# Sliding-window attention and gated FFN, gradients: the mean of dO.V without a block-sum matmul, and some of the order changed

## The chip, the cores and the metric

The kernel runs on one core of one Trainium2 chip. The metric is device time in microseconds (us), given as the median of three runs. Engines are named as in the profile: PE is TensorE's matmuls, PEld its weight loads, DVE is VectorE, ACT is ScalarE, POOL is GpSimd, SP is SyncE, which here only issues DMAs. L12 is line 12 of the kernel before.

## The reference

The forward pass mixes two branches of x (2048 rows of 512, bf16) by a gate of each row: `out = g*a + (1-g)*b` with `g = sigmoid(sum(x * gate_w))`. Branch a is attention with 32 heads of 16 lanes, in which row s sees rows s-255 to s; branch b is a FFN of width 1376 in which the gate passes a ReLU.

```
qkv = x @ wqkv
scores = q @ k.T / 4 ; keys with 0 <= i - j < 256 ; p = softmax(scores) ; a = (p @ v) @ wo
gate = relu(x @ W_gate) ; up = x @ W_up ; b = (gate * up) @ W_down
out = g * a + (1 - g) * b
results: out and the gradients of x, wqkv, wo, W_gate, W_up, W_down, gate_w for a given grad_out
```

For the gradient of the scores each query needs `dP - D`, where dP is dO.V for each key and D is the mean of dO.V under the row's softmax, which equals the sum over the 16 lanes of dO times O. D is the subject of the main part of the change.

## The kernel before

**How work is written.** Python first collects operations (an `Op` has the engines that may do it with a cost on each, the buffers it reads and writes, and a rank), then `Flow.run` plays them against its own costs, L261 on: at each moment each free engine takes the ready operation of lowest rank that finds buffers and PSUM banks, and its instructions are emitted there. So each engine's order of instructions is fixed when the program is built, and at run time each engine takes them in that order and waits where data are not there. Where PE has nothing ready and has been idle lately, a filler matmul is emitted (L1504). The ranks of PE's operations between 3.4 and 4.3 (front and back of the FFN, some weight gradients, projections) get a random part of up to 0.02 from a fixed seed (L295 to L298).

**How attention is tiled.** Four heads make a group, 4 row blocks of 128 make a sub-block of 512 rows, and a stage is one group in one sub-block: 8 groups x 4 sub-blocks = 32 stages. Each head has 32 lanes: 16 of k or q ("lo") and 16 of v or dO ("hi"). A stage of kind A (dq side: rows are keys, columns queries) and one of kind N (dk/dv side: rows are queries, columns keys) follow each other: A of stage n, then N of stage n-1. `pack_queries` and `pack_keys` (L27) cut a stage's pairs of blocks into three packs of up to 4 blocks of 128 columns; a pack is a list of segments (row block, first column block, count), and a segment is one matmul for a head. For two of the four heads a pack makes a unit, so a stage has six units.

Each unit passes twice through `slot` (L1018): first its scores (L995, "row" matmuls of 32 rows, four at a time in the array) go through Exp on ACT (L1037) and a mask on POOL (L1013), and some slots later dP is made by L995 again from the operands `dd` and `kv1`, and multiplied by p on DVE (L1043). The masks cover runs of diagonal and far blocks, one instruction a run. Sweeps (L1063, "col" matmuls of 32 or 16 columns) multiply by v, k, q and dO and sum up over the packs. All other matmuls are "den": L662 for the projections, the FFN and weight gradients, L1346 for dx, out and the second half of the FFN.

**The chain to `dd`**, once in a stage (`tasks_A1`, L1072 to L1102): a sweep makes O and the softmax sums in PSUM (`LO`); a shuffle on DVE (L1087), Ln and Exp on ACT (L1088, L1089) give the reciprocals `ri`; DVE writes `OB`, the normalised O in the hi lanes (L1090); `U = ri * qd` is made on POOL or DVE (L1092); `pr = OB * U` (L1094) on POOL or DVE. A matmul with the constant `bones` (L1096) sums pr over a head's lanes and leaves -1/16 of the sum in its lo lanes, in the PSUM bank `de`. DVE makes `dd = U * is_hi + de` (L1098). Since `kv1` holds ones in the lo lanes, the dP matmul takes D off by itself. U is also turned by a DMA transpose on SP into `R` (L1100), which N's sweeps use, rank 1. Units of kind N of stage n-1 whose queries lie in the next sub-block need `dd` and the queries of stage n.

**The last part.** `dw(c)` (L1245) makes the gradients of wqkv and wo for a quarter of the columns: SP turns the stored head rows into `RW`, then 64 matmuls of 384 columns and 16 of 512; dw(0) and dw(1) have ranks 4.05 and 4.5, dw(2) and dw(3) 4.7. `early` (L1354) makes the FFN's parts for row blocks 0 to 11 and stores them (b_d, dx_p). `final` (L1417) then loads those (`b_t`, `x_t`, L1423 and L1424) and a pair's head rows `qk` (`load_heads`, L1319, L1324: four loads of 256 KB for two row blocks, `HQ` names the queues), multiplies by the weights wT3 (loaded at L1378 by SP) and wo, and ACT, POOL and DVE add up, o and dx are stored by SP (L1444, L1450). `whole` (L1453) does blocks 12 to 15 without the store between. The loads of qk, b_t and x_t may go on the queue of SP or of ACT, whichever `Flow.run` finds free.

Of the kernel before, what the change touches and what calls it, by code (L numbers as in the profile page):

```python
# [26 lines left out]
def pack_keys(i, nt):  # L27

    packs = [[(i + 2, i, 3), (i, i, 1)], [(i + 4, i + 2, 2), (i + 1, i, 2)], [(i + 5, i + 3, 1), (i + 3, i + 1, 3)]]
    return [place([s for s in p if s[0] < nt], lambda a, b: a - b) for p in packs]  # L30
# [20 lines left out]
HOLD, WAIT = 2.5, 800  # L51
SEED = 32
SPAN, LOW, NEED, PHASE = 3413.3, 3000, 3600, 0

def t_mm(count, cols=512):
    return count * (cols / 2.4 + 3)
# [146 lines left out]
class Flow:  # L203
# [57 lines left out]
    def run(self):  # L261
# [32 lines left out]

        rnd = random.Random(SEED)  # L295
        for o in self.ops:
            if PE in o.times and o.mode != "row" and 3.4 < o.rank < 4.3:
                o.rank += rnd.uniform(0, 0.02)  # L298

        def release(ops):  # L300
# [87 lines left out]
def kernel(  # L388
# [21 lines left out]
    P = 128  # L410
# [20 lines left out]
    MASKQ, MASKV = {DVE: 450, ACTE: 600}, {DVE: 470, ACTE: 600}  # L431
    DTT = 640
    FUSED = 0
    HQ, OUTS, GLAG = (SP, ACTE), 2, 3
    COLX, ROWX = 20, 4
# [36 lines left out]
    for w in range(2):  # L472
# [3 lines left out]
                                base=16 * w + 15, pattern=[[32, 4]], channel_multiplier=-1)  # L476
    head_m = mc.tile([P, 4], F32, name="head_m")
    nc.vector.tensor_tensor(out=head_m[:], in0=lo_m[:, :, 0], in1=lo_m[:, :, 1], op=ALU.add)
    vec = mc.tile([P, 4], F32, name="vec")
# [6 lines left out]
    less_hi = vec[:, 3:4]  # L486
    bones = mc.tile([P, 4, 2, 16], BF, name="bones")
    nc.gpsimd.memset(bones[:], 0.0)
    nc.vector.tensor_scalar(bones[:, :, 0, :], bc(head_m[:], 16), -1.0 / Dh, None, op0=ALU.mult)
    g_all = mc.tile([P, NT], F32, name="g_all")  # L490
# [581 lines left out]
    def tasks_A1(n, us):  # L1072

        hg, sb = divmod(n, NSB)
        LO, de = (buf("acc") for _ in range(2))
        ri, OB, U, pr, R = (buf(nm) for nm in ("ri", "OB", "U", "pr", "R"))
        dd, qd = st["in", n][2], st["qd", n]

        def w1(a, i):
            d, k = divmod(a - 4 * sb, 4)  # L1080
            return st["k1r", n + d][:, k, 32 * i:32 * i + 32]

        def b1(segs):
            return [st["k1r", n + (s_[0] - 4 * sb) // 4] for _, s_ in segs]

        sweep(LO, us, w1, b1, False, [OB], rank=RC)
        op({DVE: t_dve(W)}, lambda e: nc.vector.stream_shuffle(ri[:], LO[:], 2 * list(range(16))), r=[LO], w=[ri], rank=RC)  # L1087
        op({ACTE: t_act(W)}, lambda e: nc.scalar.activation(ri[:], ri[:], ACT.Ln), r=[ri], w=[ri], rank=RC)  # L1088
        op({ACTE: t_scale(W)}, lambda e: nc.scalar.activation(ri[:], ri[:], ACT.Exp, scale=less_hi), r=[ri], w=[ri], rank=RC)  # L1089
        op({DVE: t_stt(W)}, lambda e: nc.vector.scalar_tensor_tensor(  # L1090
            out=OB[:], in0=LO[:], scalar=is_hi, in1=ri[:], op0=ALU.mult, op1=ALU.mult), r=[LO, ri], w=[OB], rank=RC)
        op({POOL: t_pool(W, 2), DVE: t_dve(W)}, lambda e: EN[e].tensor_tensor(  # L1092
            out=U[:], in0=ri[:], in1=qd[:], op=ALU.mult), r=[ri, qd], w=[U], rank=RC)
        op({POOL: t_pool(W, 2), DVE: DTT}, lambda e: EN[e].tensor_tensor(  # L1094
            out=pr[:], in0=OB[:], in1=U[:], op=ALU.mult), r=[OB, U], w=[pr], rank=RC)
        op({PE: t_mm(1)}, lambda e: nc.tensor.matmul(de[:], lhsT=bones[:].rearrange("p a b c -> p (a b c)"), rhs=pr[:],  # L1096
                                                     start=True, stop=True), r=[pr], w=[de], rank=RC, mode="den", keep=[dd])
        op({DVE: t_stt(W)}, lambda e: nc.vector.scalar_tensor_tensor(  # L1098
            out=dd[:], in0=U[:], scalar=is_hi, in1=de[:], op0=ALU.mult, op1=ALU.add), r=[U, de], w=[dd], rank=RC)
        dma(lambda: nc.sync.dma_start_transpose(out=R[:], in_=U[:]), r=[U], w=[R], nbytes=128 * KB, rank=1, turn=True)  # L1100
        put(OB, *divmod(hg, 2), sb, 0, 1, 2)
        st["rn", n] = R  # L1102
# [142 lines left out]
    def dw(c):  # L1245
# [16 lines left out]
        for cd in range(DC):  # L1262
            bank, dwst = buf("mm"), buf("dwst")
            mms = [mm(lambda bank=bank: bank[:, 0:3 * P], lambda t=t, cd=cd: x_r[:, t, cd * P:(cd + 1) * P],
                      lambda t=t: RW[:, t, P:4 * P]) for t in range(NT)]
            accumulate(bank, mms, [RW, x_r], DW if c < 2 else DW2, [dwst], cols=3 * P)

            def out(e, bank=bank, dwst=dwst):
# [10 lines left out]
        accumulate(bank, [mm(lambda: bank[:], lambda t=t: Or[:, t, :], lambda t=t: db_r[:, t, :]) for t in range(NT)],  # L1279
                   [Or, db_r], DWO if c < 2 else DW2, [dst])  # L1280
        op(either(W), lambda e: copy(e, dst[:], bank[:]), r=[bank], w=[dst], rank=2)
# [135 lines left out]
    def final(t, qk):  # L1417
# [4 lines left out]
        b_t, x_t = buf("b_t"), buf("x_t")  # L1422
        dma(lambda q: q.dma_start(b_t[:], b_d[t][:]), r=[b_d[t]], w=[b_t], nbytes=256 * KB, rank=3.15, on=(SP, ACTE))  # L1423
        dma(lambda q: q.dma_start(x_t[:], dx_p[t][:]), r=[dx_p[t]], w=[x_t], nbytes=256 * KB, rank=3.15, on=(SP, ACTE))  # L1424
        dxb = buf("tb")
# [107 lines left out]
```

## Time and profile before

| what | value |
|---|---|
| median of 3 runs | 848.98 us (848.01 to 849.01) |
| profiled execution, its own time | 851.36 us |
| its span, first to last instruction | 849.7 us |
| granted clock of PE, mean of the span | 0.994 |
| PE, DVE, ACT, POOL busy | 97%, 82%, 72%, 64% |
| DMA | 152.17 MB, mean 179 GB/s |
| L1096, the block-sum matmul | x32, 381 ns a record |
| L1094, the product pr | 23 on DVE (575 ns), 9 on POOL (1153 ns) |
| L1098, dd | x32 on DVE, 738 ns |

The span has three parts: up to about 40 us the first loads and projections, then attention stages with FFN and projection matmuls between them up to about 720 us (slots of L995, sweeps of L1063, the rest of PE's time filled by L662 and later L1346), and from there the end, in which PE runs L1346, the last dw and little else. A matmul's record is longer than the distance between two starts, since they are pipelined, so a matmul's price is read from starts. Idle time of an engine other than PE costs only where PE comes to wait for it.

### The profile page before, as it was taken

What the parts mean: (1) busy time and instruction counts of PE and PEld (TensorE: products, weight loads), DVE (VectorE), ACT (ScalarE), POOL (GpSimd) and SP (SyncE); (2) the same over time, 40 slices, a digit from 0 to 9 for tenths busy, and PEclk for the clock granted to TensorE, in tenths of its full rate; (3) what the DMA queues carried; (4) which work ended last, traced back from release to release, by engine and by line L of the source; (5) the groups of instructions that cost most, each with busy time, mean ns of one, the idle gap of its engine ahead of it and who ended that gap; (6) DMA issues with size and microseconds to landing.
All of it is one profiled execution on the core that took longest, in us unless ns stands there. A gap on an engine that the chain in (4) does not pass through costs nothing.

```text
span 849.7 us, 24038 instructions
## 1 busy us (share of the span) xinstructions
PE 823.5 (97%) x8722; PEld 372.8 (44%) x8722; DVE 698.6 (82%) x1278; ACT 614.8 (72%) x1244; POOL 544.0 (64%) x942
## 2 busy tenths in 40 slices
PE   8999999999999999999999999999999999999999
PEld 5433444434454544445354444443333333444444
DVE  5589899898999797999999998988989899634351
ACT  5778887797888787888888798988887877321232
POOL 6378677687798586978867685556565665122341
PEclk9999999999999999999999999999999999999999
DMA  8978565656678888878875599537656464889892
GB/s 230 227 169 207 143 159 139 140 155 156 147 197 187 171 196 176 194 171 208 192 169 154 158 222 205 147 103 153 177 147 171 138 184 154 251 255 278 245 229 60
DMA packets 317033, 152.17 MB, mean 179 GB/s; under 512 B 205233, under 2 KB 309234, under 8 KB 316274
## 3 DMA queue, kind: packets, MB, share of 16 engines
q1 hardware_dynamic: 297090, 135.69, 65.5%
q10 hardware_dynamic: 19248, 13.37, 5.3%
q0 software_dynamic: 576, 1.57, 0.8%
q8 instruction: 68, 1.11, 0.6%
q14 instruction: 51, 0.42, 0.2%
HBM read 55.02 MB, written 55.74 MB: 130 GB/s over the span
## 4 chain that ended last, share of the span: by engine, by line
PE 73%; DMA 10%; POOL 5%; DVE 5%; ACT 3%; issue 2%; SPq 1%; ACTq 0%; DVEq 0%; POOLq 0%
PE banks L662 34%; PE banks L1346 17%; PE banks L995 12%; PE banks L1063 8%; DVE arena L1043 2%; POOL arena L1013 2%; ACT arena L1037 2%; POOL arena L868 1%; DMA arena<-HD_d 1%; DMA arena<-arena 1%; DMA ffn_d<-arena 1%; DMA QD_d<-arena 1%; DMA arena<-QD_d 1%; DMA arena<-KV_d 1%; PE banks L1096 1%
## 5 line engine op out<-in xcount | busy, mean ns | idle before, releaser
L1043 DVE TENSOR_TENSOR arena<-arena,banks 128x512 bf16<-128x512 bf16 (+2 forms) x768 | 461.3, 645 | 39.0 <-PE banks L995 29.4
L1013 POOL TENSOR_SCALAR_AFFINE_SELECT arena<-arena 128x256 bf16<-128x256 bf16 (+1 forms) x736 | 350.2, 499 | 180.9 <-ACT arena L1037 163.8
L1037 ACT ACTIVATE arena<-banks 128x512 bf16<-128x512 f32 (+2 forms) x768 | 399.8, 573 | 81.4 <-PE banks L995 71.9
L662 PE MATMUL banks<-arena 128*128 128x512 bf16 (+4 forms) x1984 | 392.7, 337 | 4.7 <-DVE arena L1043 2.2
L662 PEld LDWEIGHTS <-arena 128*128 128x128 bf16 (+1 forms) x1984 | 174.0, 99 | 160.9 <-issue 61.8
L1346 PE MATMUL banks<-arena 128*128 128x512 bf16 (+1 forms) x784 | 186.6, 380 | 2.4 <-DMA arena<-wt_d 1.7
L995 PE MATMUL banks<-arena 32*128 32x384 bf16 (+2 forms) x2816 | 166.6, 277 | 8.4 <-DVE arena L1043 2.0
L995 PEld LDWEIGHTS <-arena 32*128 32x128 bf16 x2816 | 51.5, 92 | 157.7 <-issue 147.2
L640 ACT CAST arena<-banks 128x512 bf16<-128x512 f32 (+4 forms) x167 | 81.0, 497 | 53.9 <-PE banks L662 42.0
L868 POOL TENSOR_TENSOR arena<-arena 128x512 bf16<-128x512 bf16 (+1 forms) x84 | 98.4, 1176 | 20.7 <-DVE arena L863 10.8
L1346 PEld LDWEIGHTS <-arena 128*128 128x128 bf16 (+1 forms) x784 | 69.8, 97 | 93.9 <-issue 20.3
L1063 PE MATMUL banks<-arena 128*32 128x384 bf16 (+5 forms) x2816 | 103.0, 277 | 4.3 <-DMA arena<-arena 3.3
L1063 PEld LDWEIGHTS <-arena 128*32 128x32 bf16 (+1 forms) x2816 | 57.6, 94 | 42.0 <-issue 24.6
L1442 POOL TENSOR_TENSOR arena<-arena 128x512 bf16<-128x512 f32 x12 | 15.2, 1266 | 49.5 <-ACT arena L1441 27.0
L1092 POOL TENSOR_TENSOR arena<-arena 128x512 bf16<-128x512 f32 x31 | 36.1, 1165 | 9.4 <-issue 7.2
L868 DVE TENSOR_TENSOR arena<-arena 128x512 bf16<-128x512 bf16 (+1 forms) x48 | 36.7, 767 | 2.6 <-DMA ffn_d<-arena 2.2
L1446 DVE SCALAR_TENSOR_TENSOR arena<-gw_b,arena 128x512 f32<-128x512 bf16 x12 | 10.4, 865 | 25.6 <-ACT arena L1445 25.6
L1448 POOL TENSOR_TENSOR arena<-arena 128x512 bf16<-128x512 f32 x12 | 15.5, 1305 | 24.1 <-DMA out_dram<-arena 15.0
L863 DVE SCALAR_TENSOR_TENSOR arena<-arena,banks 128x512 bf16<-128x512 bf16 (+1 forms) x44 | 29.7, 677 | 0.9 <-PE banks L662 0.8
L1441 ACT ACTIVATE arena<-banks,g_all 128x512 f32<-128x512 f32 x12 | 8.1, 686 | 30.8 <-PE banks L1346 13.2
L1445 ACT COPY arena<-banks 128x512 f32<-128x512 f32 x12 | 6.9, 584 | 26.4 <-PE banks L1346 23.9
L858 ACT ACTIVATE arena<-banks 128x512 bf16<-128x512 f32 (+1 forms) x36 | 21.7, 604 | 5.4 <-PE banks L662 4.4
(92 smaller groups left out, 459.8 us busy)
## 6 DMA issues: line engine op xcount, KB each, us to landing
ffn_d<-arena SPq DMA_DIRECT2D x40, 384.0 KB
arena<-ffn_d SPq DMA_DIRECT2D x88, 128.0 KB
out_dram<-arena SPq DMA_DIRECT2D x66, 128.0 KB
arena<-HD_d ACTq DMA_DIRECT2D x31, 256.0 KB
KV_d<-arena SPq DMA_DIRECT2D x32, 128.0 KB
QD_d<-arena SPq DMA_DIRECT2D x32, 128.0 KB
arena<-KV_d SPq DMA_DIRECT2D x32, 128.0 KB
arena<-QD_d SPq DMA_DIRECT2D x32, 128.0 KB
```

The costliest lines, as they stand in the source:

```text
L640: nc.scalar.copy(out, in_)
L662: return lambda start, stop: nc.tensor.matmul(out_fn(), lhsT=lhs_fn(), rhs=rhs_fn(), start=start, stop=stop)
L858: nc.scalar.activation(q["rg"][:fs, :], gps[:fs, :], ACT.Relu)
L863: op({DVE: t_stt(W)}, lambda e, q=q, ups=ups: nc.vector.scalar_tensor_tensor(out=q["upm"][:fs, :], in0=q["rg"][:fs, :], scalar=0.0, in1=up ...
L868: op({POOL: t_pool(W, 2), DVE: DTT}, lambda e, q=q, k=k, a=a, b=b: EN[e].tensor_tensor(out=q["act"][:fs, k, :], in0=q[a][:fs, :], in1=q[b] ...
L995: nc.tensor.matmul(bank, lhsT=lt[rs, ls], rhs=rt[rs, rsl], start=True, stop=True)
L1013: nc.gpsimd.affine_select(out=v.rearrange("p h (b k) -> p h b k", b=cnt), in_=v.rearrange("p h (b k) -> p h b k", b=cnt), compare_op=ALU.i ...
L1037: op({ACTE: t_act(w)}, lambda e, h=h: nc.scalar.activation(nxt.Pt[:, h, :w], nxt.S[h][:, :w], ACT.Exp), r=[nxt.S[h]], w=[(nxt.Pt, h)], rank=0)
L1043: op({DVE: t_dve(wc)}, lambda e, h=h: nc.vector.tensor_tensor(out=cur.Pd[:, h, :wc], in0=cur.Pt[:, h, :wc], in1=cur.dP[h][:, :wc], op=ALU. ...
L1063: nc.tensor.matmul(acc[32 * i:32 * i + wt.shape[1], q0:q0 + cnt * P], lhsT=wt, rhs=m[:, i % 2, col * P:(col + cnt) * P], start=(k == 0), s ...
L1092: op({POOL: t_pool(W, 2), DVE: t_dve(W)}, lambda e: EN[e].tensor_tensor(out=U[:], in0=ri[:], in1=qd[:], op=ALU.mult), r=[ri, qd], w=[U], r ...
L1346: nc.tensor.matmul(bank[:], lhsT=l_(), rhs=r_(), start=(lo + k == 0), stop=(lo + k == n - 1))
```

## The change

- **The mean of dO.V.** `bones`, its helper `head_m`, the bank `de` and the matmul L1096 go. pr is made on POOL alone. A `stream_shuffle` on DVE moves pr by 16 lanes within each head, so that each product of a hi lane stands in a lo lane of `dd`; then DVE makes `dd = U * is_hi - dd`, both tensors in SBUF. The dP matmul with its ones in `kv1` sums the 16 single products.
- **dk/dv packs.** The three packs of kind N now hold 4, 4 and 4 blocks as before, but in seven segments instead of six, and all segments with row blocks of the next sub-block stand in the third pack. At the last sub-block the widths are 4, 4 and 1 instead of 4, 2 and 3.
- **Ranks.** The random part of PE's ranks goes. R's transpose has rank 0. dw(2) and its dWo rank like dw(0) and dw(1).
- **Last loads.** qk, b_t and x_t are issued by SP alone.

In the built order PE has 9205 matmuls where it had 8722: 512 more on the lines of L995 and L1063, 3 more fillers, 32 of L1096 fewer. POOL has 608 masks of 2 x 128 columns and 176 of 2 x 256, before 512 and 224. On SP the eight loads of wT3 and 20 of the 32 loads of qk stand ahead of the first store of o or dx; 12 loads of qk stand between such stores.

```diff
 def pack_keys(i, nt):
 
-    packs = [[(i + 2, i, 3), (i, i, 1)], [(i + 4, i + 2, 2), (i + 1, i, 2)], [(i + 5, i + 3, 1), (i + 3, i + 1, 3)]]
+    packs = [[(i + 2, i, 3), (i, i, 1)], [(i + 3, i + 1, 3), (i + 1, i, 1)], [(i + 4, i + 2, 2), (i + 1, i + 1, 1), (i + 5, i + 3, 1)]]
...
-        rnd = random.Random(SEED)
-        for o in self.ops:
-            if PE in o.times and o.mode != "row" and 3.4 < o.rank < 4.3:
-                o.rank += rnd.uniform(0, 0.02)
...
-    DTT = 640
+    DTT, SHUF = 640, 620
-    HQ, OUTS, GLAG = (SP, ACTE), 2, 3
+    HQ, OUTS, GLAG = (SP,), 2, 3
...
-    head_m = mc.tile([P, 4], F32, name="head_m")
-    nc.vector.tensor_tensor(out=head_m[:], in0=lo_m[:, :, 0], in1=lo_m[:, :, 1], op=ALU.add)
...
-    bones = mc.tile([P, 4, 2, 16], BF, name="bones")
-    nc.gpsimd.memset(bones[:], 0.0)
-    nc.vector.tensor_scalar(bones[:, :, 0, :], bc(head_m[:], 16), -1.0 / Dh, None, op0=ALU.mult)
...
-        LO, de = (buf("acc") for _ in range(2))
+        LO = buf("acc")
...
-        op({POOL: t_pool(W, 2), DVE: DTT}, lambda e: EN[e].tensor_tensor(
+        op({POOL: t_pool(W, 2)}, lambda e: EN[e].tensor_tensor(
             out=pr[:], in0=OB[:], in1=U[:], op=ALU.mult), r=[OB, U], w=[pr], rank=RC)
-        op({PE: t_mm(1)}, lambda e: nc.tensor.matmul(de[:], lhsT=bones[:].rearrange("p a b c -> p (a b c)"), rhs=pr[:],
-                                                     start=True, stop=True), r=[pr], w=[de], rank=RC, mode="den", keep=[dd])
-        op({DVE: t_stt(W)}, lambda e: nc.vector.scalar_tensor_tensor(
-            out=dd[:], in0=U[:], scalar=is_hi, in1=de[:], op0=ALU.mult, op1=ALU.add), r=[U, de], w=[dd], rank=RC)
-        dma(lambda: nc.sync.dma_start_transpose(out=R[:], in_=U[:]), r=[U], w=[R], nbytes=128 * KB, rank=1, turn=True)
+        op({DVE: SHUF}, lambda e: nc.vector.stream_shuffle(dd[:], pr[:], list(range(16, 32)) + list(range(16))),
+           r=[pr], w=[dd], rank=RC)
+        op({DVE: DTT}, lambda e: nc.vector.scalar_tensor_tensor(
+            out=dd[:], in0=U[:], scalar=is_hi, in1=dd[:], op0=ALU.mult, op1=ALU.subtract), r=[U, dd], w=[dd], rank=RC)
+        dma(lambda: nc.sync.dma_start_transpose(out=R[:], in_=U[:]), r=[U], w=[R], nbytes=128 * KB, rank=0, turn=True)
...
-            accumulate(bank, mms, [RW, x_r], DW if c < 2 else DW2, [dwst], cols=3 * P)
+            accumulate(bank, mms, [RW, x_r], DW if c < 3 else DW2, [dwst], cols=3 * P)
...
-                   [Or, db_r], DWO if c < 2 else DW2, [dst])
+                   [Or, db_r], DWO if c < 3 else DW2, [dst])
...
-        dma(lambda q: q.dma_start(b_t[:], b_d[t][:]), r=[b_d[t]], w=[b_t], nbytes=256 * KB, rank=3.15, on=(SP, ACTE))
-        dma(lambda q: q.dma_start(x_t[:], dx_p[t][:]), r=[dx_p[t]], w=[x_t], nbytes=256 * KB, rank=3.15, on=(SP, ACTE))
+        dma(lambda: nc.sync.dma_start(b_t[:], b_d[t][:]), r=[b_d[t]], w=[b_t], nbytes=256 * KB, rank=3.15)
+        dma(lambda: nc.sync.dma_start(x_t[:], dx_p[t][:]), r=[dx_p[t]], w=[x_t], nbytes=256 * KB, rank=3.15)
```

More of the change, by code (lines that the diff above doesn't have):

```diff
@@ L1 @@
 import heapq
-import random
 from contextlib import ExitStack
@@ L51 @@
 HOLD, WAIT = 2.5, 800
-SEED = 32
 SPAN, LOW, NEED, PHASE = 3413.3, 3000, 3600, 0
```

## The prediction

> **What bounds the kernel now.** I read the engine shares of the page first, then busy time by stretches, then the waits of TensorE, then single stretches of its timeline, and last the end of the run. The shares, and the stretches before and after 720 us, where attention ends (busy time of TensorE, its weight loads, VectorE, ScalarE, POOL, then granted clock, DMA share, GB/s):
>
> ```profile
> PE 823.5 (97%) x8722; PEld 372.8 (44%) x8722; DVE 698.6 (82%) x1278; ACT 614.8 (72%) x1244; POOL 544.0 (64%) x942
> ...
> 16.00:720.00 704.00, 685.36 (x7886) 307.62 (x7887) 637.90 (x1140) 573.96 (x1158) 498.81 (x883) 0.99 0.71 171
> 720.00:849.70 129.70, 125.44 (x720) 56.20 (x720) 54.58 (x122) 33.31 (x74) 35.07 (x34) 1.00 0.76 218
> ```
>
> TensorE is the bound in both stretches (685.4 of 704.0 us, 125.4 of 129.7). VectorE comes close in the first: 637.9 of 704.0, 66.1 us idle. The waits of TensorE are small, and VectorE ends most of them (us in total, times, longest):
>
> ```profile
> PE banks L662 <- DVE arena L1043: 2.2, 4, 1.4
> PE banks L995 <- DVE arena L1043: 2.0, 5, 1.2
> PE banks L995 <- DVE arena L642: 1.8, 2, 1.2
> PE banks L1346 <- DMA arena<-wt_d: 1.7, 2, 1.0
> ...
> PE banks L995 <- DVE arena L1090: 1.4, 1, 1.4
> ...
> PE banks L1096 <- DVE arena L1094: 1.0, 2, 0.5
> ```
>
> So a matmul taken out of the stream should shorten the run, if nothing else becomes late. The stream, in three places of TensorE's timeline (start, length):
>
> ```profile
> 135.63 0.38 PE L1096 MATMUL banks<-arena,bones 128*128 128x512 bf16 x1
> 135.84 1.03 PE L662 MATMUL banks<-arena 128*128 128x256 bf16 x8
> ...
> 306.62 0.40 PE L995 MATMUL banks<-arena 32*128 32x256 bf16 x8
> 306.95 1.47 PE L662 MATMUL banks<-arena 128*128 128x512 bf16 x6
> 308.35 0.40 PE L995 MATMUL banks<-arena 32*128 32x128 bf16 x8
> 308.68 0.67 PE L1063 MATMUL banks<-arena 128*32 128x384 bf16 x16
> 309.29 0.39 PE L662 MATMUL banks<-arena 128*128 128x512 bf16 x1
> ...
> 728.35 0.34 PE L995 MATMUL banks<-arena 32*128 32x384 bf16 x2
> 728.62 0.60 PE L1346 MATMUL banks<-arena 96*128 96x512 bf16 x2
> ```
>
> A record lasts 0.38 us, but the next matmul starts 0.21 us later (135.63 to 135.84): the starts are the price.
>
> **The changes, part by part.** The sum is against the profiled execution's own time, 851.36 us (span 849.7 and 1.66 around it); the median shown, 848.98, lies 2.38 below it.
>
> *Block-sum matmul out.* 32 matmuls (L1096, one a stage) x 0.21 us = -6.7 us. In front of them TensorE also stood still: its groups by form give 1.6 us for L1096. In order as it is, that can vanish, or the next instruction waits instead: -1.6 to 0, I take half, -0.8. The freed PSUM bank I count at nothing, since no wait shown is for a bank.
>
> *Recut of the dk/dv packs.* One segment more in each of 32 stages: the built order has 512 more matmuls and weight loads on lines 995 and 1063, with the same columns. Each stage has four score passes with the longer pack and two sweeps. A pass of 384 columns in one segment took 0.27 us (728.35 to 728.62), one of 512 in two 0.33 (306.62 to 306.95). Taking off 160 and 213 ns of columns (2.4 a ns, from the six 512-column matmuls in 1.40 us) leaves 0.11 and 0.12: a segment more costs 0.01 us. The sweep of 16 matmuls, four segments and 1152 columns, took 0.61, so 0.13 over: at most 0.03 a segment, and 0.01 if, like the pass, it is mostly the change of mode. 32 x (4 x 0.0075 + 2 x 0.01) = +1.6 us. Ends: 0, and all of the remainder charged to segments, 32 x (4 x 0.06 + 2 x 0.03) = +9.6; the pair of passes says it is near the low one. The masks become 96 of 435 ns for 48 of 645: POOL +10.8 us. ScalarE's and VectorE's widths at the border move (4,2,3 blocks to 4,4,1) at the same sum, nothing. The second scores of a dk/dv unit now need the next stage's dd in units 5 and 6 instead of 3 to 6; the waits on L1098 that this frees are 0.4 us on TensorE, left at nothing.
>
> *VectorE's new work.* Per stage it loses L1098 (0.738) and, in 23 of 32 stages, the product L1094 (0.575), together 1.15 us. It gains a shuffle of bf16 from SBUF, not shown before: between 0.51 (L952, one source in SBUF) and 0.73 (L1087, the fp32 shuffle from PSUM). I take 0.65, nearer the same operation. It gains a combined multiply-subtract with both tensors in SBUF: between 0.68 (L863) and 1.44 (the longest L1446, which has both tensors in SBUF; median 0.75). I take 0.75. So +0.25 a stage, +8 us, with ends +1 and +33; the new order shifts evictions between the engines for another +1. Idle falls from 66 to 57 us. The waits of TensorE on VectorE sum to 8.2 without L1096; taken to grow as idle shrinks, 8.2 x 66/57 = 9.5: +1.3 us (0 to +8.7, where the end of +33 leaves 32 us idle).
>
> The row that speaks against this step is L1094 on VectorE, both inputs in SBUF: 412 to 1358 ns, median 554, where L1098, with one input in PSUM, stayed within 732 to 748. The Trainium skill, GPSIMD Engine Reference, Key points, says that GpSimd shares SBUF interfaces with VectorE and contends with its instructions of two SBUF inputs; the spread agrees. By that rule alone each new multiply-subtract could go at 1.36, which makes VectorE's idle 37 us instead of 57 and the step +6.4 us instead of +1.3.
>
> *The product always on POOL.* 23 x 1.153 = +26.5 us, with the masks +37, and POOL had 205 us idle in the first stretch (704.0 - 498.8): nothing by itself, since the one TensorE wait that POOL ended by this product was 0.3 us. If the cover is gone, the shuffle waits in VectorE's queue and holds the products L1043 behind it: the first rival.
>
> *Order dealt anew.* The random part of the ranks goes, R's transpose has rank 0, and dw(2) and its dWo rank as dw(0) and dw(1). Nothing is added on TensorE but 3 fillers (29 for 26), +0.6. The switches of mode stay, 898 for 896. What can be dealt otherwise is TensorE's idle time of the first stretch, 18.6 us, and the clock: 0.994 granted, 5.1 us. A quarter of both either way is -6 to +6; the value is +0.6.
>
> *Loads on SP alone.* 51 issues move from ScalarE's queue to SP's: 31 of qk, 12 of b_t, 8 of x_t, some 0.43 us each (21.8 us). From 730 to 797 us SP issued for 21.3 of 67 us and would have 42. Now SP is blocked there behind stores. Two lines of the waits of SP's queue (total, times, longest), and three of TensorE's timeline near 765 us:
>
> ```profile
> SPq L1444 <- POOL arena L1442: 20.4, 8, 5.4
> ...
> SPq L1450 <- POOL arena L1448: 9.0, 4, 3.9
> ...
> 764.17 0.59 PE L1346 MATMUL banks<-arena 128*128 128x512 bf16 x2
> 765.45 2.86 PE L1346 MATMUL banks<-arena 128*128 128x512 bf16 x12 [0.68 <-DMA arena<-wt_d]
> 769.27 1.02 PE L1346 MATMUL banks<-arena 128*128 128x512 bf16 x4 [0.97 <-DMA arena<-wt_d]
> ```
>
> The reader is to see that TensorE's late loads are those of wT3, which SP issued between such stores (749 to 765 us). In the built order all eight of them now come ahead of the first store of o; 20 of the 32 qk loads too, and 12 behind stores. So -1.0, of the 1.7 that these waits cost; ends -2.4 (all DMA waits on L1346) and +10.2 (four tiles each late by the mean wait of L1444, 20.4/8 = 2.55). The set-up loses a few small operations (bones 1.8 us on VectorE); the first loads hide them, and without them it is 2 us at most.
>
> Sum: -6.7 - 0.8 + 1.6 + 1.3 + 0.6 - 1.0 = **-5.0 us**. 851.36 - 5.0 = 846.4 for an execution like the profiled one, and 2.38 less for the median: **844.0**.
>
> **The rivals.**
> *Slower: VectorE held behind POOL.* The place is the shuffle, first in VectorE's in-order queue until POOL has written pr. For it: SP's transpose of U waited 29.4 us in 24 stages for POOL, so POOL runs behind the written order by about 1.2 us there; and VectorE has 66 us idle. Against it: VectorE itself waited only 0.8 us for U. A wait of w a stage leaves 57 - 32w idle. At w = 0.6 (38 us idle) TensorE's waits are 8.2 x 66/38 = 14.2, +6.0 in place of +1.3: 848.7, the point where the gain is gone. At w = 0.9, 28 us idle, 19.3, +11.1: 853.8. Chance 0.20.
> *Slower: SP's queue late at the end.* The +10.2 end in place of -1.0: 844.0 + 11.2 = 855.2. For it: the 20.4 us above. Against it: 1.7 us is all that SP's waits cost TensorE so far, and five of the eight qk are loaded ahead. 0.08.
> *The order is dealt worse.* +6 instead of +0.6, 849.4, no change: 0.10 (with the deciding w of the first rival); beyond it, three more windows of half clock at 1.7 us each, 854.5: 0.06.
> *Better than forecast,* the low ends of the order and of the last part: 844.0 - 6.6 - 1.4 = 836.0: 0.04.
>
> **How the numbers follow.** Forecast 0.52 (its own range 839 to 847, from half of the order's quarter and the ends of the small terms). Within 0.2% (1.7 us either way, about what a measurement of this kernel can tell from no change) are 847.3 to 850.7. Faster 0.52 + 0.04 = 0.56; same 0.10; slower 0.20 + 0.08 + 0.06 = 0.34. The range takes the slower cases up to 855 and leaves out what lies beyond and the far low end: 838.5 to 855.
>
> **What would show it.** Right: matmul starts on TensorE with no L1096 and a first stretch some 5 us shorter; shuffle near 0.65 and multiply-subtract near 0.75 us; VectorE 705 to 709 us busy, POOL near 580; idle time of VectorE ahead of the shuffle below 0.3 us a stage; waits on wT3 gone. Wrong: VectorE waiting 0.6 us or more a stage for pr, TensorE's waits on L1043 above 10 us, a multiply-subtract above 1.1, more half-clock windows, or qk loads that end TensorE's waits past 720 us.

## The result, and the profile after

The changed kernel takes 862.08 us (median; 859.97 to 865.48) against 849.0 us for the kernel before on the same chip (848.01 to 854.07): 1.0136 times as long, 95% interval 1.0102 to 1.0170. Forecast were 844.0 us and a range up to 855. Its profiled execution took 859.97 us.

The page of the kernel after, engine shares, and then the busy time by stretches (TensorE, its weight loads, VectorE, ScalarE, POOL, granted clock, DMA share, GB/s):

```profile
span 858.1 us, 24993 instructions
...
PE 822.7 (96%) x9205; PEld 385.3 (45%) x9205; DVE 710.8 (83%) x1320; ACT 616.4 (72%) x1240; POOL 584.8 (68%) x1013
...
16.00:720.00 704.00, 674.78 (x8235) 315.17 (x8236) 641.70 (x1161) 569.69 (x1147) 531.16 (x940) 1.00 0.71 167
```

TensorE's work was to shrink so that the span shrinks. Its busy time is nearly unchanged (822.7 for 823.5) and the span is 8.4 us longer: TensorE stands still for more of it. In the stretch up to 720 us its idle time is 29.2 us (704.00 - 674.78), before 18.6, at a clock that is not worse. The sweeps of attention say where the length is; their one line (L1063 before, L1051 after: the change shortens the code by 12 lines there) ends with the first and last start. Kernel before:

```profile
L1063 PE MATMUL banks<-arena x2816: 216/273/337, 41.9 to 738.6; 128*32 128x384 bf16 x53, 128*32 128x256 bf16 x48, 128*32 128x128 bf16 x41, 128*16 128x256 bf16 x17
```

Kernel after:

```profile
L1051 PE MATMUL banks<-arena x3072: 216/272/400, 42.3 to 750.8; 128*32 128x384 bf16 x71, 128*32 128x128 bf16 x56, 128*16 128x128 bf16 x40, 128*32 128x256 bf16 x25
```

Attention ends 12.2 us later (738.6 to 750.8). From there to the end of the span it is 107.3 us instead of 111.1: the last part got shorter. So the loss lies in attention alone. TensorE's idle time there stands ahead of the score and dP passes. The costliest groups, kernel before (busy us, mean ns of one, then the idle time just before them and what ended most of it):

```profile
L995 PE MATMUL banks<-arena 32*128 32x384 bf16 (+2 forms) x2816 | 166.6, 277 | 8.4 <-DVE arena L1043 2.0 <-DVE arena L642 1.8 <-DVE arena L1090 1.4
```

and after, where L983 is that line, with the groups of the multiply-subtract and of the product on POOL:

```profile
L983 PE MATMUL banks<-arena 32*128 32x128 bf16 (+2 forms) x3072 | 172.7, 267 | 19.6 <-DVE arena L1031 6.8 <-ACT arena L1025 6.1 <-DVE arena L1086 3.8
...
L1082 POOL TENSOR_TENSOR arena<-arena 128x512 bf16<-128x512 bf16 x32 | 37.3, 1166 | 2.1 <-DVE arena L1080 0.8 <-DVE arena L938 0.8 <-DVE arena L1078 0.5
...
L1086 DVE SCALAR_TENSOR_TENSOR arena<-arena,vec 128x512 bf16<-128x512 bf16 x32 | 29.6, 926 | 0.0
```

Idle ahead of the passes went from 8.4 to 19.6 us; only 3.8 of that is for the new multiply-subtract (L1086). Most of the rest is for the products (L1031) and exponentials (L1025) of every slot, which the change does not touch. So a reading that looks at the new instructions alone finds a third of it.

Two of the lines that were to show the steps. The shuffle:

```profile
L1084 DVE STREAM_SHUFFLE arena<-arena x32: 675/684/695, 49.8 to 727.4; 128x512 bf16<-128x512 bf16 x32
its engine sat idle before it (us, times) until:
  POOL arena L1082: 3.4, 2
```

and the multiply-subtract (ns: shortest, median, longest):

```profile
L1086 DVE SCALAR_TENSOR_TENSOR arena<-arena,vec x32: 742/819/2333, 51.0 to 728.6; 128x512 bf16<-128x512 bf16 x32
```

The shuffle is as forecast and waits for POOL 0.1 us a stage. The multiply-subtract is not: what a long one looks like is in three engines' timelines of one stretch (start, length, and in brackets the idle time before it and its releaser). VectorE:

```profile
456.46 2.33 DVE L1086 SCALAR_TENSOR_TENSOR arena<-arena,vec 128x512 bf16<-128x512 bf16 x1
458.71 1.87 DVE L1031 TENSOR_TENSOR arena<-arena,banks 128x512 bf16<-128x512 bf16 x3
```

POOL:

```profile
455.17 4.50 POOL L1001 TENSOR_SCALAR_AFFINE_SELECT arena<-arena 128x256 bf16<-128x256 bf16 x10
```

TensorE:

```profile
458.85 0.28 PE L983 MATMUL banks<-arena 32*128 32x256 bf16 x2 [0.80 <-DVE arena L1086]
```

While POOL makes ten masks in a row, the instruction with both inputs in SBUF lasts three times its shortest; the products of VectorE around it, with one input in PSUM, last 0.62 us each (1.87 for three), and the mean of that shape over the whole run is 0.680. TensorE waits 0.80 us.

### The profile page after: what moved, and what is told of

The parts are those of the page before. It is cut to its first block, busy times and chain, and to the rows that moved or that the text cites. A ratio compares the mean times of both kernels' runs of the same rounds, so it can differ in the third digit from the quotient of the medians.

```text
span 858.1 us, 24993 instructions
## 1 busy us (share of the span) xinstructions
PE 822.7 (96%) x9205; PEld 385.3 (45%) x9205; DVE 710.8 (83%) x1320; ACT 616.4 (72%) x1240; POOL 584.8 (68%) x1013
## 3 DMA queue, kind: packets, MB, share of 16 engines
q8 instruction: 72, 1.18, 0.6%
## 4 chain that ended last, share of the span: by engine, by line
PE 67%; DMA 8%; POOL 8%; DVE 7%; issue 4%; ACT 3%; SPq 2%; DVEq 0%; POOLq 0%; ACTq 0%
PE banks L650 29%; PE banks L1334 17%; PE banks L983 12%; PE banks L1051 8%; DVE arena L1031 4%; POOL arena L1001 4%; DMA arena<-QD_d 3%; POOL arena L856 2%; ACT arena L1025 2%; DMA ffn_d<-arena 1%; SPq L911 1%; DMA arena<-HD_d 1%; POOL arena L1082 1%; DMA arena<-in_B_W_gate_dram 1%; POOL arena L1080 1%
## 5 line engine op out<-in xcount | busy, mean ns | idle before, releaser
L1031 DVE TENSOR_TENSOR arena<-arena,banks 128x512 bf16<-128x512 bf16 (+3 forms) x768 | 460.3, 647 | 28.6 <-PE banks L983 21.1
L1001 POOL TENSOR_SCALAR_AFFINE_SELECT arena<-arena 128x256 bf16<-128x256 bf16 (+1 forms) x784 | 361.7, 486 | 143.8 <-ACT arena L1025 138.5
L1025 ACT ACTIVATE arena<-banks 128x512 bf16<-128x512 f32 (+3 forms) x768 | 398.5, 571 | 80.3 <-PE banks L983 69.9
L983 PE MATMUL banks<-arena 32*128 32x128 bf16 (+2 forms) x3072 | 172.7, 267 | 19.6 <-DVE arena L1031 6.8
L983 PEld LDWEIGHTS <-arena 32*128 32x128 bf16 x3072 | 62.0, 92 | 171.1 <-issue 154.2
L856 POOL TENSOR_TENSOR arena<-arena 128x512 bf16<-128x512 bf16 (+1 forms) x87 | 103.8, 1196 | 23.6 <-DMA ffn_d<-arena 9.3
L1051 PE MATMUL banks<-arena 128*32 128x128 bf16 (+5 forms) x3072 | 103.4, 268 | 1.4 <-DVE arena L1031 0.5
L1051 PEld LDWEIGHTS <-arena 128*32 128x32 bf16 (+1 forms) x3072 | 61.9, 94 | 44.0 <-issue 22.8
L1430 POOL TENSOR_TENSOR arena<-arena 128x512 bf16<-128x512 f32 x12 | 15.7, 1307 | 72.5 <-DMA arena<-b_d 56.5
L1080 POOL TENSOR_TENSOR arena<-arena 128x512 bf16<-128x512 f32 x31 | 36.2, 1166 | 10.2 <-issue 7.3
L1082 POOL TENSOR_TENSOR arena<-arena 128x512 bf16<-128x512 bf16 x32 | 37.3, 1166 | 2.1 <-DVE arena L1080 0.8
L856 DVE TENSOR_TENSOR arena<-arena 128x512 bf16<-128x512 bf16 (+1 forms) x45 | 32.1, 722 | 5.1 <-DMA ffn_d<-arena 3.9
L630 DVE CAST arena<-banks 128x512 bf16<-128x512 f32 (+2 forms) x45 | 24.7, 560 | 6.3 <-PE banks L650 4.3
L1086 DVE SCALAR_TENSOR_TENSOR arena<-arena,vec 128x512 bf16<-128x512 bf16 x32 | 29.6, 926 | 0.0
L939 ACT ACTIVATE arena<-arena,vec 128x512 bf16<-128x512 bf16 x27 | 19.6, 724 | 12.3 <-DMA arena<-QD_d 12.2
```

What stands on the lines that cost most here:

```text
L856: op({POOL: t_pool(W, 2), DVE: DTT}, lambda e, q=q, k=k, a=a, b=b: EN[e].tensor_tensor(out=q["act"][:fs, k, :], in0=q[a][:fs, :], in1=q[b] ...
L983: nc.tensor.matmul(bank, lhsT=lt[rs, ls], rhs=rt[rs, rsl], start=True, stop=True)
L1001: nc.gpsimd.affine_select(out=v.rearrange("p h (b k) -> p h b k", b=cnt), in_=v.rearrange("p h (b k) -> p h b k", b=cnt), compare_op=ALU.i ...
L1025: op({ACTE: t_act(w)}, lambda e, h=h: nc.scalar.activation(nxt.Pt[:, h, :w], nxt.S[h][:, :w], ACT.Exp), r=[nxt.S[h]], w=[(nxt.Pt, h)], rank=0)
L1031: op({DVE: t_dve(wc)}, lambda e, h=h: nc.vector.tensor_tensor(out=cur.Pd[:, h, :wc], in0=cur.Pt[:, h, :wc], in1=cur.dP[h][:, :wc], op=ALU. ...
L1051: nc.tensor.matmul(acc[32 * i:32 * i + wt.shape[1], q0:q0 + cnt * P], lhsT=wt, rhs=m[:, i % 2, col * P:(col + cnt) * P], start=(k == 0), s ...
```

## The experiments

Two theories at first. *Deal* (theory 1 below): the fixed order of instructions, dealt anew when the random part of the ranks goes, is worse than the one before, and the edits in the arithmetic matter little. *VectorE* (theory 2): the two instructions that VectorE gains (shuffle and multiply-subtract, stretched by POOL) hold up the passes. Theory 3 was that the loads on SP alone cost time at the end. Ratios are to the kernel before on the same chip, with 95% intervals. The recut of the packs, the rank of R's transpose and the product on POOL alone were not run by themselves. Line numbers shift by a few lines between kernels.

### The order alone

The kernel before without the random part of the ranks, all work the same:

```diff
-        rnd = random.Random(SEED)
-        for o in self.ops:
-            if PE in o.times and o.mode != "row" and 3.4 < o.rank < 4.3:
-                o.rank += rnd.uniform(0, 0.02)
```

> The kernel before with the random part of the ranks taken out, nothing else; the work of every engine is that of before. Theory 1 (the order as dealt is what costs: row passes of TensorE wait behind instructions of ScalarE and VectorE that stand in queue behind late DMAs): 853 to 862 us, with TensorE's waits on line 995 well above the 7 us of before. Theory 2 (the new work in the chain to dd costs: a multiply-subtract of 0.93 us, the shuffle, the product on POOL): the same as before, 847 to 851. Theory 3 (the last loads on SP's queue cost): the same as before.

Measured: 862.35 us, 1.0153 (1.0122 to 1.0184). This one edit loses as much as the whole change, as theory 1 has it and a little above its range. Attention ends at 748.2 us instead of 738.6, the rest is as long as before (111.1). No wait stands out: the idle time ahead of the passes is 13.5 us instead of 8.4, and its releasers are many:

```profile
L990 PE MATMUL banks<-arena 32*128 32x384 bf16 (+2 forms) x2816 | 166.1, 276 | 13.5 <-ACT arena L1032 2.8 <-DVE arena L763 2.0 <-DVE arena L1093 1.3
```

The counterpart puts the random part (seed 32) back into the kernel after:

```diff
+SEED = 32
...
+        rnd = random.Random(SEED)
+        for o in self.ops:
+            if PE in o.times and o.mode != "row" and 3.4 < o.rank < 4.3:
+                o.rank += rnd.uniform(0, 0.02)
```

> The changed kernel with the random part of the ranks put back, the seed that before has; all other edits stay. Theory 1: another deal of the same work, anywhere from 848 to 864 us, a difference from the 862 of the changed kernel of several us either way, carried by TensorE's waits on line 983 of the page (46 us above the price of starts in the changed kernel, 33 in before). Theory 2: 858 to 864 us, as the chain is the same, with the multiply-subtract near 0.93 us again. Theory 3: 858 to 864 us.

Measured: 862.5 us, 1.0161 (1.0126 to 1.0196). It does not bring the time back. With another set of operations the same random numbers are only another deal. That asks how deals spread, and whether a random part helps as such. Other seeds in the kernel before, one number changed:

```diff
-SEED = 32
+SEED = 1
```

> The kernel before with seed 1 in place of 32 for the random part of the ranks; same work, another deal of the order. Theory 1a (the deal of before is a lucky one, and every other deal of this work is some 10 us longer): 856 to 864 us, attention ending 7 us or more later than the 738.6 of before. Theory 1b (a random part of any kind helps, and what hurts is to do without): 847 to 852 us.

> The kernel before with seed 2. As for seed 1: theory 1a 856 to 864 us, theory 1b 847 to 852 us; the distance between the two seeds shows how much a deal alone moves the time.

> A fifth deal of the kernel before. Those so far without seed 32: 862.4, 861.2, 856.5. If seed 32 is one of the best of many: 855 to 863; at 850 or less a deal like it would be common.

and in the kernel after:

> The changed kernel with a random part of seed 1. Theory 1a: like the changed kernel and its run with seed 32, 856 to 866 us. Theory 1b: between those already measured and 850. If the work of the edits themselves is worth the 5 us that the sum gave, the three deals of the changed kernel lie on the mean some 5 us below the three of before that aren't seed 32.

> A fourth deal of the changed kernel. Those so far: 862.1, 862.5, 867.8. If deals of this kernel lie together: 860 to 868; one at 852 or less would show that the edits leave room for as good a deal as before's.

| deal | before's work | idle ahead of passes | attention ends | after's work | idle ahead of passes | attention ends |
|---|---|---|---|---|---|---|
| as it stands | 1 (seed 32) | 8.4 us | 738.6 | 1.0136 (no seed) | 19.6 us | 750.8 |
| no seed / seed 32 | 1.0153 | 13.5 | 748.2 | 1.0161 | 19.2 | 746.6 |
| seed 1 | 1.0118 (1.0080 to 1.0157) | 14.1 | 749.4 | 1.0223 (1.0163 to 1.0282) | 21.9 | 753.6 |
| seed 2 | 1.0100 (1.0063 to 1.0136) | 12.2 | 746.7 | 1.0081 (1.0050 to 1.0112) | 16.9 | 745.8 |
| seed 3 | 1.0099 (1.0063 to 1.0135) | 12.0 | 743.9 | | | |

Every other deal of the old work is 1.0 to 1.5% slower than the one shown, with a random part (seeds 1, 2 and 3) as without; their mean is 1.0118. The four deals of the changed work have the mean 1.0150; seeds 1 and 2 of them, at 867.83 and 855.29 us, lie outside what was expected for deals of this kernel. The order before is the fastest of five, whether by choice or by luck is not known, and the change gave it up. Against ordinary deals the edits together cost +0.3%, and the deals within either column scatter by 0.3 and 0.6% (standard deviation), so that this +0.3% is not told apart from nothing; a gain of 0.6%, as forecast, does not show either.

What makes the other deals slower is not resolved. Attention ends 8.5 us later in the four of the old work (mean 747.05), and the idle time ahead of the passes is 4.6 us longer (mean 12.95 against 8.4). But the traces of all seeded runs and of the one without a seed in the kernel before lack some 1.4% of TensorE's matmul records, those of the kernels before and after none, and the place of a missing record counts as idle. Waits of over 0.15 us ahead of the passes sum to 7.7 us in the kernel before and to 9.1 to 10.6 in these four, so the waits that can be told make 1 to 3 us of the 8.5. There are also more fillers, 28 to 40 for 26. The comparison of before and after (8.4 and 19.6) is free of this.

### The matmul and VectorE's work, in the old order

To take the deal out, the operations were kept for the plan and only what they emit was changed, so TensorE's order stays that of the kernel before. First the arithmetic of the change: no block-sum matmul, shuffle and multiply-subtract on VectorE where `dd` was made.

```diff
-        op({PE: t_mm(1)}, lambda e: nc.tensor.matmul(de[:], lhsT=bones[:].rearrange("p a b c -> p (a b c)"), rhs=pr[:],
-                                                     start=True, stop=True), r=[pr], w=[de], rank=RC, mode="den", keep=[dd])
-        op({DVE: t_stt(W)}, lambda e: nc.vector.scalar_tensor_tensor(
-            out=dd[:], in0=U[:], scalar=is_hi, in1=de[:], op0=ALU.mult, op1=ALU.add), r=[U, de], w=[dd], rank=RC)
+        op({PE: t_mm(1)}, lambda e: None, r=[pr], w=[de], rank=RC, mode="den", keep=[dd])
+
+        def ddf(e):
+            nc.vector.stream_shuffle(dd[:], pr[:], list(range(16, 32)) + list(range(16)))
+            nc.vector.scalar_tensor_tensor(out=dd[:], in0=U[:], scalar=is_hi, in1=dd[:], op0=ALU.mult, op1=ALU.subtract)
+
+        op({DVE: t_stt(W)}, ddf, r=[U, de, pr], w=[dd], rank=RC)
```

> The order of the kernel before is kept on every engine; only the block-sum matmul is left out of TensorE's stream and VectorE does a shuffle and a multiply-subtract where it did one multiply-add. Theory 1: 6.7 us of starts fall away and VectorE gains 32 x (0.68 + 0.93 - 0.74) = 28 us, of which it had 66 idle; the order has no room planned for these, so 843 to 849 us. Theory 2: slower than before, 853 to 862 us, with the waits of row passes on the multiply-subtract at 4 us or more. Theory 3: faster by about 6, 842 to 844.

Measured: 865.82 us, 1.0175 (1.0129 to 1.0220). In the old order it is theory 2 that holds, above its range, and theory 1's 843 to 849 us are refuted. Then the same without the shuffle (`in1=pr[:]`), one VectorE instruction for one:

> The order of before, with the block-sum matmul left out and nothing in its place: dd is made by one multiply-subtract from pr as it stands, so the mean of dO.V is not taken off and the gradient of x and wqkv is not the reference's. It shows what 32 starts on TensorE are worth by themselves. If a start is the price, as the forecast had it: 6.7 us and up to 1.6 of waits less, 841 to 844 us. If the stream only waits elsewhere instead: 846 to 850 us.

Measured: 855.65 us, 1.0059 (1.0037 to 1.0082), slower than either range. And without the second SBUF input, a scale of U:

```diff
+        op({DVE: t_stt(W)}, lambda e: nc.vector.tensor_scalar(
+            dd[:], U[:], is_hi, None, op0=ALU.mult), r=[U, de, pr], w=[dd], rank=RC)
```

> As b_nosum (the order of before, no block-sum matmul), but VectorE makes dd by a scale of U alone, one tensor in SBUF, 0.45 to 0.51 us as lines 952 and 954 of before; the mean of dO.V is not taken off. If the stretched multiply-subtract was what ate the gain: 841 to 845 us. If 32 starts less are worth nothing in this order: 847 to 852.

Measured: 846.45 us, 1.0013 (0.9981 to 1.0045). The three in one view each, the idle time ahead of the passes and the last VectorE instruction of `dd`. Shuffle and multiply-subtract:

```profile
L995 PE MATMUL banks<-arena 32*128 32x384 bf16 (+2 forms) x2816 | 168.8, 279 | 29.4 <-DVE arena L1100 18.4 <-ACT arena L951 2.0 <-DVE arena L1043 1.9
...
L1100 DVE SCALAR_TENSOR_TENSOR arena<-arena,vec 128x512 bf16<-128x512 bf16 x32 | 30.0, 939 | 1.1
```

Multiply-subtract alone:

```profile
L995 PE MATMUL banks<-arena 32*128 32x384 bf16 (+2 forms) x2816 | 168.8, 277 | 16.3 <-DVE arena L1097 6.8 <-DVE arena L1090 1.7 <-ACT arena L1037 1.0
...
L1097 DVE SCALAR_TENSOR_TENSOR arena<-arena,vec 128x512 bf16<-128x512 bf16 x32 | 29.9, 935 | 0.0
```

Scale of one source:

```profile
L995 PE MATMUL banks<-arena 32*128 32x384 bf16 (+2 forms) x2816 | 167.8, 278 | 13.2 <-DVE arena L1097 3.1 <-ACT arena L1037 1.7 <-DVE arena L1090 1.3
...
L1097 DVE TENSOR_SCALAR arena<-arena,vec 128x512 bf16<-128x512 bf16 x32 | 17.6, 549 | 0.0
```

The last one is the cleanest test of "a matmul less is 0.21 us less": 32 matmuls are out, the VectorE instruction that makes `dd` is shorter in the mean than before (549 ns for L1098's 738), and the time is unchanged, as expected if 32 starts less are worth nothing in this order. The interval allows a gain of 0.2%, 1.6 us, where the prediction had taken off 7.5. The starts did go, but TensorE comes earlier to passes whose inputs come no earlier: waits of over 0.15 us ahead of the passes sum to 9.6 us where they were 7.7, ahead of the sweeps to 6.6 where they were 4.0 (5.3 of it for the transposed `R`, before 3.3), together +4.6 us. (The whole idle time, 13.2 for 8.4 ahead of the passes, can't be compared, as this trace too lacks 116 of 8690 matmul records.) The granted clock of the profiled execution was lower too, 0.990 for 0.994, which is 3.4 us. So 6.7 us of starts and 1.6 us of waits of L1096 itself went, 4.6 and 3.4 came, and the span went from 849.7 to 849.2. Over all executions the clock was 0.9918 in the mean, that of the kernel before on the same chip 0.9939, some 1.8 us. That later inputs and clock ate the gain is argued from these sums; no run separates the two, and why the clock was lower is not known.

The middle one has the longer VectorE instruction, 935 for 549 ns, and took 1.0059 for 1.0013, some 4 us. That is not yet the price of the second SBUF input: the two are different operations, their intervals overlap, and the clock of the middle one was 0.9890 in the mean, that of the kernel before on its chip 0.9933, some 3.7 us by itself. The first gives the shuffle where the plan has no room for it: the passes wait 18.4 us for L1100 instead of 6.8 for L1097, 1.0059 to 1.0175.

### VectorE's work, in the new order

The same two in the kernel after: shuffle not emitted and the multiply-subtract fed from pr; and a one-source scale in place of both.

```diff
-        op({DVE: SHUF}, lambda e: nc.vector.stream_shuffle(dd[:], pr[:], list(range(16, 32)) + list(range(16))),
-           r=[pr], w=[dd], rank=RC)
+        op({DVE: SHUF}, lambda e: None, r=[pr], w=[dd], rank=RC)
         op({DVE: DTT}, lambda e: nc.vector.scalar_tensor_tensor(
-            out=dd[:], in0=U[:], scalar=is_hi, in1=dd[:], op0=ALU.mult, op1=ALU.subtract), r=[U, dd], w=[dd], rank=RC)
+            out=dd[:], in0=U[:], scalar=is_hi, in1=pr[:], op0=ALU.mult, op1=ALU.subtract), r=[U, dd, pr], w=[dd], rank=RC)
```

> The order of the changed kernel with the shuffle left out and dd made by one multiply-subtract from pr as it stands, so the mean of dO.V is not taken off and the gradients of x and wqkv aren't the reference's. VectorE has 32 x 0.68 = 22 us less. If VectorE's load in attention makes TensorE's longer waits (17 us on VectorE against 9 before): 854 to 858 us. If the time goes by the order as dealt, with VectorE's load of little weight: 859 to 863 us.

> As a_noshuf (the order of the changed kernel, no shuffle), with the multiply-subtract replaced by a scale of U alone; the mean of dO.V is not taken off. If the stretched multiply-subtract holds TensorE's row passes in the changed kernel: 848 to 856 us. If the order as dealt is the rest: 857 to 862, with waits on ScalarE and on line 1031 as before.

Measured: 861.23 us, 1.0124 (1.0061 to 1.0188) without the shuffle, 855.43 us, 1.0094 (1.0062 to 1.0126) with the scale alone. In an order that was planned with the shuffle, leaving it out gives nothing that can be told (1.0136 to 1.0124; VectorE's busy time falls from 710.8 to 698.3 us, since the multiply-subtract got longer, 1071 ns in the mean). With the scale alone the time lies at the edge of the range for a multiply-subtract that holds the passes (848 to 856), but the kernel before was faster on that chip too (847.38 us). By the ratio, 0.4% of the loss may be VectorE's new work, though the intervals overlap. Even with both gone, 1% of loss stays, and the idle time ahead of the passes with it (in waits of over 0.15 us 18.2 us, in the kernel after 19.0):

```profile
L983 PE MATMUL banks<-arena 32*128 32x128 bf16 (+2 forms) x3072 | 171.2, 267 | 20.6 <-ACT arena L1025 6.8 <-DVE arena L1031 5.3 <-DVE arena L1085 2.6
```

So VectorE's new work is not the main cause in the changed kernel. 6.8 us of the idle time are ended by ACT's exponentials, which do not read `dd`.

What then stands ahead of these passes? One example of the kernel after, VectorE and TensorE near 327 us:

```profile
326.63 0.42 DVE L856 TENSOR_TENSOR arena<-arena 128x512 bf16<-128x512 bf16 x1 [2.78 <-DMA ffn_d<-arena]
326.97 0.48 DVE L1031 TENSOR_TENSOR arena<-arena,banks 128x128 bf16<-128x128 bf16 x2
```

```profile
327.31 0.37 PE L983 MATMUL banks<-arena 32*128 32x256 bf16 x3 [1.98 <-DVE arena L1031]
```

An instruction of the FFN (L856) stands first in VectorE's queue and waits 2.78 us until a store has read its buffer; the products behind it, which attention needs, wait with it, and TensorE after them for 1.98 us. The view of waits names the product, which was itself held up. Whether an order has such a neighbour in a bad place is decided when it is dealt. This is one place; how much of the idle time is of this kind was not shown.

### The last part

Loads on SP alone, in the kernel before:

```diff
-    HQ, OUTS, GLAG = (SP, ACTE), 2, 3
+    HQ, OUTS, GLAG = (SP,), 2, 3
...
-        dma(lambda q: q.dma_start(b_t[:], b_d[t][:]), r=[b_d[t]], w=[b_t], nbytes=256 * KB, rank=3.15, on=(SP, ACTE))
+        dma(lambda q: q.dma_start(b_t[:], b_d[t][:]), r=[b_d[t]], w=[b_t], nbytes=256 * KB, rank=3.15, on=(SP,))
```

(and x_t alike).

> The kernel before with qk, b_t and x_t issued by SP alone. The order is that of before until these loads begin, near 730 us. Theories 1 and 2: 846 to 851 us, the stretch past 720 us within 2 us of that of before. Theory 3: 853 us or more, with TensorE waiting for qk past 730 us.

The ranks of dw(2) and its dWo alone, in the kernel before:

```diff
-            accumulate(bank, mms, [RW, x_r], DW if c < 2 else DW2, [dwst], cols=3 * P)
+            accumulate(bank, mms, [RW, x_r], DW if c < 3 else DW2, [dwst], cols=3 * P)
...
-                   [Or, db_r], DWO if c < 2 else DW2, [dst])
+                   [Or, db_r], DWO if c < 3 else DW2, [dst])
```

> The kernel before with the ranks of dw(2) as in the change and nothing else. If early dw(2) shortens the end by itself: last part 106 to 109 us, 845 to 849. If it only moves matmuls from the end into attention: attention later by as much as the end is shorter, 848 to 853.

Both together, and the same measured a second time:

> The kernel before with the last loads on SP alone and the ranks of dw(2) as in the change; its attention keeps the order of before up to about 600 us. The changed kernel's last part was 3.6 us shorter than before's (107.4 and 111.0), where the loads on SP alone made it longer (117.7). If the two edits belong together (dw(2) done early takes DMA and matmuls out of the end): last part 105 to 109 us, time 844 to 849. If SP's queue costs whatever the rest: 855 to 859.

> The kernel of b_sp_dw again, with more rounds. If its shorter end (106.7 us after the last sweep, 111.0 before) carries to the time: a ratio of 0.994 to 0.998 with an interval below 1. If the first run was within what deals of the clock do: 0.998 to 1.002.

And the kernel after with the loads on both queues again:

> The changed kernel with the last loads on the queues of SP and ScalarE again; the order of TensorE is that of the changed kernel until these loads begin. If SP's queue alone cost time at the end (theory 3), the part after the last sweep falls from 107.4 us and the time by 3 us or more, to 859 or less. If the loads are hidden either way, as the forecast took it: 860 to 864 us, the last part 105 to 110 us.

| kernel | ratio | attention ends | from there to the end | fillers |
|---|---|---|---|---|
| before | 1 | 738.6 | 111.1 | 26 |
| SP alone | 1.0098 (1.0066 to 1.0130) | 736.6 | 117.7 | 44 |
| dw(2) alone | 1.0136 (1.0083 to 1.0190) | 741.9 | 117.7 | 51 |
| both | 0.9972 (0.9944 to 1.0001), again 0.9969 (0.9946 to 0.9993) | 738.3, 738.8 | 106.7, 106.2 | 27 |
| after | 1.0136 | 750.8 | 107.3 | 29 |
| after, SP and ACT | 1.0339 (1.0271 to 1.0406) | 753.6 | 125.3 | 68 |

SP alone took 857.51 us, as theory 3 expected, but not with its sign: TensorE never waits for qk there. dw(2) alone, with 861.31, is slower than either range. The kernel after with both queues, with 879.69, is too; a lower clock is part of that (0.987 in the mean of its runs, 0.993 in the kernel before, some 5 of the 29 us).

Neither edit is good or bad by itself. Alone, each leaves TensorE with nothing ready by the plan, which then emits fillers in a row. SP alone, TensorE's timeline at the end; behind this row it waits 2.5 us more for the head rows of the last dw:

```profile
827.14 5.13 PE L1504 MATMUL banks<-arena,ident 128*128 128x512 bf16 x23 [0.16 <-issue]
```

dw(2) alone, a row of fillers, then a wait on a load of wT3:

```profile
758.24 5.35 PE L1504 MATMUL banks<-arena,ident 128*128 128x512 bf16 x24
763.43 2.57 PE L1346 MATMUL banks<-arena 128*128 128x512 bf16 x10
769.33 70.85 PE L1346 MATMUL banks<-arena 128*128 128x512 bf16 x320 [3.32 <-DMA arena<-wt_d]
```

With both, TensorE waits 0.2 us for a load past 730 us and has a single stretch of 67 us of L1346. Why the plan leaves it without work with one edit and not with two was not followed further. The stretch:

```profile
757.58 67.33 PE L1346 MATMUL banks<-arena 128*128 128x512 bf16 x311
```

This version of the kernel before, with these two edits and nothing else of the change, is the fastest here: 0.3% less than the kernel before (847.86 us against 851.02 in the second measurement, whose interval lies below 1; that of the first just reaches it).

## Why the prediction was wrong

- **Order dealt anew: the step that failed.** It was put at +0.6 us with ends of -6 and +6, from a quarter of the idle time and the clock of the order shown. The runs: without the random ranks alone +1.53%, about 13 us; over other deals of the old work +1.18%, about 10 us. The mistake was to take the order shown for a sample from the middle. It is the lowest of five, and its trace alone does not show that. The rival "dealt worse" had the right sign, but went past +6 only by the clock (three more windows of half clock, 854.5 us); the profiled executions had 0.996 after and 0.994 before. Over all four executions after, the clock was 0.991, before on the other chips 0.993 to 0.994, so some 2 us of the 13 may be clock. In what way the other orders lose their 10 us stays open. One part of this step came out well: the sweeps' wait for `R`, 3.3 us before, is gone after.
- **Block-sum matmul out, -6.7 and -0.8: failed too.** "The starts are the price" holds for TensorE's busy time and not for the run: in the unchanged order the 32 matmuls less gave 1.0013 (0.9981 to 1.0045), while waits ahead of passes and sweeps grew by 4.6 us and a lower clock took 3.4 in the profiled execution. The condition put ahead of the step, "if nothing else becomes late", was the whole question; the passes that need `dd`, `R` and the products were late next.
- **VectorE's new work, +1.3: mis-sized.** Shuffle 0.684 us for 0.65: right. Multiply-subtract 0.926 us in the mean for 0.75. In the old order the longer instruction went with some 4 us, which a lower clock may explain as well. The scaling of TensorE's waits with VectorE's idle time failed with it: VectorE's idle time up to 720 us fell only from 66.1 to 62.3 us (704.00 - 641.70), by which the waits of 8.2 would be 8.7; TensorE's waits on VectorE came to 17.1, 11.1 of them on the products L1031, which is the sign of being wrong that the prediction had set at 10. VectorE's share does not say which of its instructions stand ahead of a product. The spread of L1094 (412 to 1358 ns) was the row to go by, and the sum did not. The Trainium skill, GPSIMD Engine Reference, Key points, says that GpSimd shares SBUF interfaces with VectorE and contends with its instructions of two SBUF inputs; the trace agrees, 742 to 2333 ns beside POOL's work, and by it alone the forecast would have been 849.1 us.
- **First rival, VectorE held behind POOL at the shuffle: wrong.** 3.4 us over 32 stages, 0.1 a stage, where 0.6 decides.
- **Recut, +1.6: wrong by its size, harmless.** In the kernel after, eight row matmuls take a median of 0.329 us up to the next other matmul and ten of the same columns take 0.332, and sweeps of 24 and of 28 matmuls both take 0.772: 128 passes longer by 0.003 us are 0.4 us. The rate in the step, 2.4 columns a ns, is not that of the six matmuls it names (3072 columns in 1.40 us are 2.2); with 2.2 the two passes leave 0.09 and 0.10, so already there a segment costs next to nothing. Long rows without a change of mode do give 2.4 (311 matmuls of up to 512 columns in 67.33 us).
- **Product always on POOL, 0: right.** POOL is 584.8 us busy, near 580, and ended 3.4 us of VectorE's idle time by this product.
- **Loads on SP, -1.0: right in sign for the change,** whose last part is 3.8 us shorter, though in the kernel before it needs dw(2) early as well, which was not in the step: alone it costs 1%. The second rival (SP's queue late) did not come: the wait of SP's queue that took 20.4 us on L1444 is 1.2 us on its successor, and no wait of TensorE on wT3 is left. In the kernel after:

```profile
SPq L1468 <- DVE arena L1462: 6.9, 2, 6.0
SPq L1438 <- POOL arena L1436: 3.4, 5, 0.9
...
SPq L1432 <- POOL arena L1430: 1.2, 3, 0.7
```

In sum: some +10 us for the order that was given up, a gain of 7.5 us that did not come, and the multiply-subtract's stretch. What the edits are worth against ordinary deals, +0.3% in the mean, and how it divides among them stays open, since it is smaller than the scatter.

## What to carry to other kernels

Where a program fixes each engine's order from ranks with a chosen seed, an edit must be judged against several deals of both versions, since a single deal moved the time by more here (1%) than the edits together; and the trace of one deal did not show how good a deal it was. A matmul taken out of a 97% busy TensorE was worth nothing here, where what the next passes wait for came no earlier. Edits at the end of a program (which queue loads, which weight gradients run early) are to be tried in pairs: here two losses of 1% made a gain of 0.3%.

## What the runs showed of the hardware

- The same VectorE instruction form (`scalar_tensor_tensor`, 128x512 bf16) took 732 to 748 ns with one input in PSUM, in 32 stages with POOL busy for 64% of the span, and 742 to 2333 ns (mean 926) with both inputs in SBUF. The eight longest of these, 984 ns and more, all lie beside two or more POOL instructions; others that do took no longer than 750. A scale with one SBUF source was stretched as well: median 372, mean 549, longest 1348 ns in the old order, longest 4682 in the new; the five in the old order with no POOL instruction beside them took 337 to 345.
- A shuffle of 128x512 bf16 within SBUF took 675 to 695 ns in all 32 stages, with POOL busy for 68% of the span. The Trainium skill, VectorE: DVE Perf Modes, section on the perf-mode tier table, gives the shuffle one speed alone, about 2400 ns for 2048 elements; an estimate from it for 512 is 600 ns, and the trace has 684.
